# Attention with head mixing and two gated layers on one core: attention's result kept in SBUF as operands, and another order of scores and loads

## The chip, the cores and the metric

One core of one Trainium2 chip. The time is device microseconds (us) of one execution, from the median of the runs; less is better. All arithmetic is fp32; the second stage splits each fp32 operand into a high and a low fp32r part and multiplies three times.

## The reference, cut to what matters

```
scores = q @ k.T / 8                       # 4 batches, 12 heads, 448 rows, head size 64
scores = einsum('bhij,hg->bgij', scores, w_pre)
attn = exp(scores - max); attn /= sum(attn) + 1e-9
attn = einsum('bhij,hg->bgij', attn, w_post)
x = (attn @ v) as [1792 tokens, 768]
x = (sigmoid(x @ w_gate) * (x @ w_val)) @ w_out      # d_ff 1536
out = relu(x @ w_in2) ** 2 @ w_out2                  # d_ff 2048
```

## The kernel before

**Attention** (`attention`, L64) goes through 17 row tiles, of 60 rows (the first), 100 or 120 rows, four to a batch (five in the first). A tile has a step for each 20 rows: 3, 5 or 6 steps, 92 in all. The *scores* of a tile are computed per head pair (six pairs p): TensorE writes `turn`, ScalarE copies it to `e` (L211), and two DMAs (L215) spread `e` into the tile `g`, in which rows and heads lie as the head mixing wants them. All twelve DMAs into `g` must land before the next tile's first *premix* (L226, TensorE, `g` to `ps_m`). A step is: premix, maximum (L242, VectorE), exponent (L250, ScalarE, one step later), normal (L258), postmix (L277, TensorE, three steps later, copied into `ap` by VectorE, L295). The *values* of a tile (L312, two halves of three head pairs) come in the fourth and fifth step of the next tile. The scores of tile n+1 are placed among the steps of tile n by the numbers `spread`. There are two PSUM tiles `turn`, used in turn by scores, postmix and values.

`valued` (L321) copies the values' result to `xo` (L326) and stores it in the DRAM tensor `xs` (L328). Loads are on SP's queue as well: `q_load` (L182), `k_load` (L178, one tile a head pair) and `v_load` (L190, half of a batch's heads in one DMA). SP issues its DMAs in order.

**The second stage** (`mlp`, L671) multiplies 2x2 block matrices with 7 products instead of 8. Its weights come as raw 64-bit words, are turned into the block combinations (`convert`: loads L761, ScalarE L765 and L768, VectorE L771, GpSimd L777, combinations L799, stores L806 to DRAM, here `gv`, `wo`, `wi`) in 34 *groups*, and are loaded again as units of six blocks (L856) which ScalarE and VectorE split (L872, L875) for TensorE (`job`, L901: 1430 jobs of three matmuls). The first 12 groups, `gv`, are those of w_gate and w_val; the first 252 jobs use one for each 21 jobs. Operand parts of x are made by L885 and L888; x itself is read from `xs` by `stored` (L976).

**What sets the order.** `Feed` is a planner that runs when the program is built: every task has a due job number, costs per engine and buffers from `Stock`s, and tasks are written into the engines' queues between the steps of attention (`feed.step`) and, after it, until all are out (`feed.finish`). A group may begin once `hold` jobs are out:

```
hold = max(0, min((count[0] - BEFORE) * PACE, need))
```

`cells` are buffers of 128x448; `widen` gives more of them as attention's pools close (`after_scores`, `after_mixes`, `after_all`).

Of the kernel before, what the change touches and what calls it, by code (L numbers as in the profile page):

```python
# [25 lines left out]
LAG = 3  # L26
NA = 4
EB = 4
KB = 10
UT = 6  # L30


# [28 lines left out]
    return rows  # L61


def attention(tc, feed, q, k, v, w_pre, w_post, xs, B, H, S, D):  # L64

# [30 lines left out]
    def last_of(n):  # L98
        return n + 1 == NT or tiles[n + 1][0] != tiles[n][0]

    with ExitStack() as ctx, ExitStack() as mix, ExitStack() as low, ExitStack() as left:
        kw = dict(side="right")
        one = ctx.enter_context(tc.tile_pool(name="a_one", bufs=1, **kw))
        pv = ctx.enter_context(tc.tile_pool(name="a_v", bufs=4, **kw))
        po = ctx.enter_context(tc.tile_pool(name="a_o", bufs=2, **kw))
        pa = ctx.enter_context(tc.tile_pool(name="a_a", bufs=NA, **kw))
        pg = low.enter_context(tc.tile_pool(name="a_g", bufs=1, **kw))
        ps_t = ctx.enter_context(tc.tile_pool(name="ps_t", bufs=1, space=PSUM, **kw))
# [69 lines left out]
        def k_load(b, p):  # L178
            k_t[b, p] = pk.tile([P, S], F32, tag="k", name="k")
            nc.sync.dma_start(out=k_t[b, p], in_=k[b, p])  # L180

        def q_load(n, p0=0, p1=NP):  # L182
            if p0 == 0:
                q_t[n] = p2.tile([P, NP, IM], F32, tag="q", name="q")
            n0, isz = sum(sizes[:n]) * H * D, sizes[n]
            n1 = n0 + isz * H * D
            x = q[n0:n1].rearrange("(d p i) -> d p i", d=P, p=NP)
            nc.sync.dma_start(out=q_t[n][:, p0:p1, :isz], in_=x[:, p0:p1])

        def v_load(b, i):  # L190
            v_t[b, i] = pv.tile([P, 2 * VP, JT, D], F32, tag="v", name="v")
            nc.sync.dma_start(out=v_t[b, i], in_=v[b, i])

        def scores(n, p, ps, early=False):
# [107 lines left out]
        def values(n, i):  # L302

            b, i0, i1, length, lead = tiles[n]
            c = length * GI
            ps = next_turn()
            x = mixed_of(n).rearrange("p (j y g) c -> p j y g c", y=2, g=H)
            vt = v_t[b, i]
            for m in range(VP):
                for j in range(JT):  # L310
                    for o in range(2):
                        nc.tensor.matmul(  # L312
                            ps[o * D : (o + 1) * D, 0, m * 2 * c : (m + 1) * 2 * c],
                            lhsT=vt[:, 2 * m + o, j],
                            rhs=x[:, j, :, (i * VP + m) * 2 + o],
                            start=j == 0,
                            stop=j == JT - 1,
                        )
            return lambda: valued(n, i, ps)

        def valued(n, i, ps):  # L321
            b, i0, i1, length, lead = tiles[n]
            w = i1 - i0
            xo = po.tile([P, VP, IM], F32, tag="xo", name="xo")
            x = ps[:, 0, : VP * length * STEP].rearrange("p (m w) -> p m w", m=VP)[:, :, lead : lead + w]
            nc.scalar.copy(xo[:, :, :w], x)  # L326
            to = xs[b][i * VP * P : (i + 1) * VP * P, i0:i1].rearrange("(m p) n -> p m n", p=P)
            nc.sync.dma_start(out=to, in_=xo[:, :, :w])  # L328
            if last_of(n) and (i + 1) * VP == NP:
                feed.fire(("x", b))  # L330


        plan = {s: [] for s in range(NS + 12)}
        for n in range(1, NT):
            s0, s1 = starts[n - 1], starts[n]
            spread = {3: (1, 1, 0), 5: (2, 2, 1, 1, 0), 6: (2, 2, 1, 1, 0, 0)}[s1 - s0]
            p = NP - sum(spread)
            for m, x in enumerate(spread):
                for _ in range(x):
                    plan[s0 + m].append(("scores", n, p))  # L340
                    p += 1
# [18 lines left out]
            scores(1, p, next_turn())  # L360
        q_load(2)

        k_next = {}
        for n in range(NT):
            if not last_of(n) or n + 1 == NT:
                continue
            b = tiles[n][0] + 1
            first_free = KB - NP
            for p in range(NP):
                at = starts[n - 1] + 1 + p // 2 if p < first_free else starts[n - 1] + 2 + p // 2  # L370
                k_next.setdefault(at, []).append((b, p))
        v_next = {2: [(0, 0)], 3: [(0, 1)]}
        for n in range(NT):
            if last_of(n) and n + 1 < NT:
                v_next[starts[n] + 2] = [(tiles[n + 1][0], 0)]
                v_next[starts[n] + 3] = [(tiles[n + 1][0], 1)]

        closed = False
        for s in range(NS + 12):
            if s < NS:  # L380
                premix(s)
            if 2 <= s < NS + 2:
                normal(s - 2)
            if s < NS:
                maximum(s)
            if 1 <= s <= NS:
                exponent(s - 1)
                if s == NS:
                    mix.close()
                    low.close()  # L390
                    feed.widen(1)
                    feed.free["PE"] = feed.now
            after = []
            if LAG <= s < NS + LAG:
                after.append(postmix(s - LAG))
            for x in k_next.get(s, ()):
                k_load(*x)
            for x in v_next.get(s, ()):
                v_load(*x)
            units = plan[s]  # L400
            for f, *x in units:
                if f == "values":
                    after.append(values(*x))
                    while len(after) > 1:
                        after.pop(0)()
            for f, *x in units:
                if f == "scores":
                    if after:
                        after.pop(0)()
                    n, p = x  # L410
                    scores(n, p, next_turn())
                    if p == NP - 1 and n + 2 < NT:
                        q_load(n + 2)
                    if n == NT - 1 and p == NP - 1:
                        left.close()
                        closed = True
                        feed.widen(0)
            for f in after:
                f()
            if 3 <= s < NS:  # L420
                feed.step(3.8)
            elif s >= NS:
                feed.step(1.5)
# [3 lines left out]
LAT = 0.15  # L427
FAR = 2.0
SLOW = 8.0
BEFORE = 12  # L430
PACE = 34
MARGIN = 1.5
PRODUCTS = ("a1", "d5", "b6", "a2", "b7", "d3", "b4")
OUTER = ("y2", "x1", "x6", "x7", "x4", "z5", "z3")
# [49 lines left out]
class Feed:  # L484
# [53 lines left out]
    def gate(self, key):  # L538
        t = Task(None, (), 0, 0)
        self.writer[key] = self.gates[key] = t  # L540

    def fire(self, key):
        t = self.gates.pop(key)
# [124 lines left out]
SP = ("SP", 0.36, False)  # L668


def mlp(ctx, tc, xs, wg, wv, wo, wi2, wo2, out):  # L671

# [1 line left out]


    feed = Feed(tc)
    NX, N = len(xs), xs[0].shape[1]
    DM = out.shape[0]  # L680
    KD = DM // P
    tiles = {"wg": wg, "wv": wv, "wo": wo, "wi2": wi2, "wo2": wo2}
# [6 lines left out]
    def pool(name, bufs, **kw):  # L689
        return ctx.enter_context(tc.tile_pool(name=name, bufs=bufs, reuse_waits="tile", **kw))  # L690
# [5 lines left out]
        for _ in range(n):  # L696
            feed.stock(cells, pool(f"m_c{feed.count}", 1, side="left"), 1)

    feed.stock(raws, pool("m_r", 2, side="left"), 2)
    feed.stock(ys, pool("m_y", 2, side="left"), 2)  # L700
    widen(10)
    dram = pool("m_dram", 1, space=DRAM)

    def after_scores():
        widen(12)
        feed.stock(w32s, pool("m_w30", 2, side="left"), 2)
        feed.stock(ws, pool("m_w0", 1, side="left"), 1)

    def after_mixes():
        feed.stock(w32s, pool("m_w31", 1, side="left"), 1)  # L710
        feed.stock(ws, pool("m_w1", 1, side="left"), 1)
        widen(20)
        for n in range(4):
            feed.stock(seeded if n < 2 else banks, pool(f"m_ps{n}", 1, space=PSUM, side="left"), 1)

    def after_all():
        feed.stock(ws, pool("m_w2", 1, side="left"), 1)
        widen(49)
        for n in range(4, 8):
            feed.stock(banks, pool(f"m_ps{n}", 1, space=PSUM, side="left"), 1)  # L720

    feed.wide = [after_scores, after_mixes, after_all]
    KG = max(K1, K2)
    spill = [dram.tile([KG * P, 2 * N], F32, name=f"spill{i}") for i in range(2)]

    def cell(dtype=F32):
        return Buf(cells, [P, N], dtype, "c")

    for b in range(NX):
        feed.gate(("x", b))  # L730


    count = [0]
# [429 lines left out]
    def middle(m, c, o):  # L1163
        x2[m, c] = o

    layer(lambda m, c, need: stored(xs[c], ("x", c), m, 0, need), gated, gv, so, K1, spill[0], 16, middle, True)
    layer(
        lambda m, c, need: x2[m, c],
        squared,
# [11 lines left out]
@with_exitstack  # L1181
def whole(ctx, tc, q, k, v, w_pre, w_post, wg, wv, wo, wi2, wo2, out):
    B, H, S, D = k.shape[0], 2 * k.shape[1], k.shape[3], k.shape[2] // 2
    DM = out.shape[0]
    dram = ctx.enter_context(tc.tile_pool(name="dram", bufs=1, space=DRAM))
    xs = [dram.tile([DM, S], F32, name=f"xs{b}") for b in range(B)]
    with tc.manual_schedule():
        feed = mlp(ctx, tc, xs, wg, wv, wo, wi2, wo2, out)
        attention(tc, feed, q, k, v, w_pre, w_post, xs, B, H, S, D)
        feed.finish()  # L1190


# [50 lines left out]
```

## Time and profile before

| | us |
|---|---|
| median of 3 runs | 1404.83 (1395.96 to 1408.46) |
| the profiled execution | 1398.87 |
| its span, first to last instruction | 1397.1 |

The page gives busy time by engine, the span in 40 slices, waits and the chain that ended last. TensorE has work in 89% of the span, but the first third is attention with many short matmuls and waits, and the rest is one long stream of 4290 matmuls of the second stage. A difference of about 1% (14 us) is what a measurement of this kernel can tell from no change.

### The profile page before, as it was taken

The numbers are of one execution on the slowest core, as the hardware profiler recorded it, in microseconds if no ns is written. First come the engines' busy times: TensorE is split into PE (matmuls) and PEld (weight loads), VectorE is DVE, ScalarE is ACT, GpSimd is POOL, SyncE is SP. The second block draws the span as 40 slices with busy tenths as digits, with TensorE's granted clock in tenths as the row PEclk, the third lists the DMA queues.
The fourth block names the chain that finished last, engine by engine and source line by source line (L and its number), as shares of the span: only waits on it lengthen the run. The fifth ranks groups of instructions, "written<-read, shape, count | busy, mean of one in ns | idle before, by whom it ended". The sixth has DMA issues, their size and how long they took to land.

```text
span 1397.1 us, 31155 instructions
## 1 busy us (share of the span) xinstructions
PE 1249.2 (89%) x12474; PEld 1043.0 (75%) x12474; DVE 879.2 (63%) x1399; ACT 736.6 (53%) x1351; POOL 288.9 (21%) x380
## 2 busy tenths in 40 slices
PE   4786787778688799999999999999999999999998
PEld 1454455545356678798899889999888999999998
DVE  2464465556366665568756599957688556898612
ACT  3564465455466454566555664764556435436620
POOL 3132222233233222321323300123313000000000
PEclk8898898999899999999999999999999999999999
DMA  5667657776676558788678861266775534352222
GB/s 152 192 220 215 193 190 233 227 208 211 187 234 217 170 194 289 243 272 273 224 268 271 281 195 57 64 219 194 266 270 175 156 110 144 99 161 57 57 85 79
DMA packets 138540, 263.93 MB, mean 189 GB/s; under 512 B 31964, under 2 KB 87836, under 8 KB 138396
## 3 DMA queue, kind: packets, MB, share of 16 engines
q1 hardware_dynamic: 137786, 261.39, 58.8%
q8 instruction: 98, 1.61, 0.5%
q10 hardware_dynamic: 610, 0.55, 0.1%
q14 instruction: 46, 0.38, 0.1%
HBM read 157.64 MB, written 64.68 MB: 159 GB/s over the span
## 4 chain that ended last, share of the span: by engine, by line
PE 58%; DVE 3%; ACT 1%; issue 1%; DMA 1%; DVEq 0%; SPq 0%; ACTq 0%
PE ps L901 58%; DVE w L875 2%; DVE c L917 1%; ACT w L872 1%; DVE c L888 0%; DMA wo<-y 0%; DMA w<-wi 0%; ACT raw L765 0%; DMA spill<-c 0%; ACT c L885 0%; DVE c L1052 0%; ACT c L925 0%; ACT ps L925 0%; ACT c L927 0%; DVE y L771 0%
## 5 line engine op out<-in xcount | busy, mean ns | idle before, releaser
L901 PE MATMUL ps<-c,w 128*128 128x448 f32 x4290 | 890.9, 369 | 24.4 <-DVE w L875 11.2
L901 PEld LDWEIGHTS ps<-c,w 128*128 128x128 f32 x4290 | 808.9, 189 | 105.4 <-DVE w L875 19.5
L875 DVE TENSOR_TENSOR w<-w,w 128x768 fp32r<-128x768 f32 x189 | 193.4, 1027 | 173.3 <-ACT w L872 169.7
L777 POOL TENSOR_TENSOR y<-y,raw 128x384 int32<-128x384 int32 x136 | 153.4, 1149 | 430.6 <-DVE y L771 156.5
L872 ACT CAST w<-w 128x768 fp32r<-128x768 f32 x189 | 156.8, 833 | 135.6 <-PE ps L901 118.6
L242 DVE TENSOR_REDUCE nm<-ps_m 128x2 f32<-128x896 f32 (+1 forms) x92 | 98.4, 1070 | 173.8 <-PE ps_m L226 173.4
L888 DVE TENSOR_TENSOR c<-c 128x448 fp32r<-128x448 f32 x280 | 166.1, 637 | 26.1 <-ACT c L885 23.0
L885 ACT CAST c<-c 128x448 fp32r<-128x448 f32 x280 | 144.0, 566 | 58.9 <-DVE c L917 52.4
L226 PE MATMUL ps_m<-g,wp 64*64 64x448 f32 (+1 forms) x720 | 96.7, 594 | 84.8 <-DMA gv<-y 26.2
L917 DVE TENSOR_TENSOR c<-ps,c 128x448 f32<-128x448 f32 x172 | 106.4, 622 | 88.5 <-PE ps L901 65.6
L211 ACT COPY e<-turn 120x896 f32<-120x896 f32 (+1 forms) x96 | 86.8, 908 | 136.6 <-issue 63.5
L277 PEld LDWEIGHTS turn<-wn,a 64*64 64x64 f32 x5040 | 113.7, 145 | 53.8 <-issue 49.7
L262 POOL TENSOR_SCALAR wn<-wq,sm 128x60 f32<-128x60 f32 x180 | 75.2, 432 | 334.7 <-DVE sm L259 232.9
L203 PE MATMUL turn<-k,q 64*64 64x448 f32 (+3 forms) x776 | 106.1, 603 | 18.0 <-DVE ap L295 12.2
L277 PE MATMUL turn<-wn,a 64*64 64x60 f32 x5040 | 113.5, 233 | 7.5 <-issue 7.5
L226 PEld LDWEIGHTS ps_m<-g,wp 64*64 64x64 f32 (+1 forms) x720 | 25.3, 141 | 123.4 <-issue 85.4
L250 ACT ACTIVATE a<-ps_m,nm 128x448 f32<-128x448 f32 x180 | 113.0, 640 | 6.9 <-DVE nm L242 6.1
L917 DVE TENSOR_TENSOR c<-c 128x448 f32<-128x448 f32 x184 | 112.8, 646 | 2.2 <-PE ps L901 0.6
L295 DVE COPY ap<-turn 128x960 f32<-128x960 f32 x88 | 101.4, 1152 | 19.7 <-PE turn L277 19.2
L925 ACT COPY c<-ps 128x448 f32<-128x448 f32 x128 | 67.6, 533 | 72.9 <-PE ps L901 70.1
L312 PE MATMUL turn<-ap,v 128*64 128x120 f32 (+2 forms) x1632 | 84.6, 261 | 1.3 <-DVE ap L295 1.3
L312 PEld LDWEIGHTS turn<-ap,v 128*64 128x64 f32 x1632 | 77.4, 139 | 4.0 <-DVE ap L295 1.4
(40 smaller groups left out, 491.8 us busy)
## 6 DMA issues: line engine op xcount, KB each, us to landing
w<-gv SPq DMA_DIRECT2D x84, 384.0 KB
g<-e SPq DMA_DIRECT2D x108, 210.0 KB
raw<-in_wo SPq DMA_DIRECT2D x56, 384.0 KB
w<-wi SPq DMA_DIRECT2D x56, 384.0 KB
w<-wo SPq DMA_DIRECT2D x49, 384.0 KB
wo<-y SPq DMA_DIRECT2D x42, 384.0 KB
g<-e SPq DMA_DIRECT2D x84, 175.0 KB
gv<-y SPq DMA_DIRECT2D x36, 384.0 KB
```

The lines of the kernel that those rows point to most:

```text
L203: nc.tensor.matmul(ps[c:c1, o, :S], lhsT=q_t[n][r, p, c:c1], rhs=kt[r], start=True, stop=True)
L226: nc.tensor.matmul(ps[u * HP : (u + 1) * HP, y, :S], lhsT=wp[r], rhs=g_of[n % 2][r, 2 * t + u], start=True, stop=True,)
L250: nc.scalar.activation(a[:, y], ps[:, y, :S], AF.Exp, bias=nm[:, y : y + 1], accum_out=sm[:, y : y + 1])
L277: nc.tensor.matmul(out[c : c + HP, u, j // 2, y], lhsT=a[r, y, j * HP : (j + 1) * HP], rhs=wn[r, y].rearrange("p g i -> p (g i)"), start=True,
L312: nc.tensor.matmul(ps[o * D : (o + 1) * D, 0, m * 2 * c : (m + 1) * 2 * c], lhsT=vt[:, 2 * m + o, j], rhs=x[:, j, :, (i * VP + m) * 2 + o] ...
L777: e.tensor_tensor(out=y3, in0=y3, in1=of(raw.tile.bitcast(I32)[:, :, 0])[:, i], op=ALU.add)
L872: e.copy(dst.tile[:, 0], flat())
L875: e.tensor_tensor(out=dst.tile[:, 1], in0=flat(), in1=dst.tile[:, 0].bitcast(F32), op=ALU.subtract)
L885: e.copy(hi.tile, src.tile)
L888: e.tensor_tensor(out=lo.tile, in0=src.tile, in1=hi.tile.bitcast(F32), op=ALU.subtract)
L901: e.matmul(bank.tile, lhsT=a[k], rhs=x[l], start=start and n == 0, stop=stop and n == 2, skip_group_check=more,)
L917: e.tensor_tensor(out=out.tile, in0=a.tile, in1=b.tile, op=op)
```

## The change

Attention's result no longer goes through DRAM. Each head pair of each batch has a `cells` buffer of its own (24 of them) from the first tile of its batch (`Feed.take`); `valued` writes into it by three ScalarE copies for each half where one went to `xo`, and the second stage's operand tasks read these buffers as their source. `xs`, its 34 stores and the 24 loads of x are gone.

The scores of the next tile stand two a step in each tile's first three steps. Loads of k and v are issued in the fourth step and later, after the step's scores; v comes in six DMAs a batch of 256 KB instead of two of 768 KB. A tile of q lies in one piece per partition (100-row tiles had six pieces of 400 B). The k pool has 9 buffers instead of 10, the v pool 8 smaller ones.

Of the planner's numbers, `BEFORE` goes from 12 to 8, `PACE` from 34 to 30, the first planned step from 3 to 9. At the start there is one buffer for raw weights and one for their combinations (two before), the second of each comes at `after_scores`; the cells at the start are 27 (10), then 4 (12), 18 (20) and 42 (49) more: 91 as before, of which x holds up to 24.

```diff
-KB = 10
+KB = 9
+VB = 8
...
+                x = p2.tile([P, NP * IM], F32, tag="q", name="q")
+                q_t[n] = x[:, : NP * sizes[n]].rearrange("p (h i) -> p h i", h=NP)
...
         def v_load(b, i):
-            v_t[b, i] = pv.tile([P, 2 * VP, JT, D], F32, tag="v", name="v")
+            v_t[b, i] = pv.tile([P, 2, JT, D], F32, tag="v", name="v")
...
-            nc.scalar.copy(xo[:, :, :w], x)
-            to = xs[b][i * VP * P : (i + 1) * VP * P, i0:i1].rearrange("(m p) n -> p m n", p=P)
-            nc.sync.dma_start(out=to, in_=xo[:, :, :w])
+            for m in range(VP):
+                to = feed.x[b][i * VP + m]
+                if i0 == 0:
+                    feed.take(to)
+                nc.scalar.copy(to.tile[:, i0:i1], x[:, m])
+                if last_of(n):
+                    feed.fire(to)
...
-            spread = {3: (1, 1, 0), 5: (2, 2, 1, 1, 0), 6: (2, 2, 1, 1, 0, 0)}[s1 - s0]
+            spread = (2, 2, 2) if n > 1 else (2,)
...
             for p in range(NP):
+                loads[starts[n - 3 + p // 3] + 3 + min(p % 3, starts[n - 2 + p // 3] - starts[n - 3 + p // 3] - 4)].append((k_load, b, p))
+            for i in range(NP):
+                loads[starts[n] + 3 + i // 2].append((v_load, b, i))
...
-            if 3 <= s < NS:
+            for f, *x in loads[s]:
+                f(*x)
+            if 9 <= s < NS:
                 feed.step(3.8)
...
-BEFORE = 12
-PACE = 34
+BEFORE = 8
+PACE = 30
...
+    def take(self, b):
+        del b.stock.line[bisect_left(b.stock.line, b.serial)]
+        _, _, b.pool = heapq.heappop(b.stock.free)
+        shape, dtype, name = b.make
+        b.tile = b.pool.tile(shape, dtype, tag="x", name=name)
...
+    feed.x = [[Buf(cells, [P, N], F32, "x") for _ in range(KD)] for _ in range(NX)]
...
-    layer(lambda m, c, need: stored(xs[c], ("x", c), m, 0, need), gated, gv, so, K1, spill[0], 16, middle, True)
+    layer(lambda m, c, need: feed.x[c][m], gated, gv, so, K1, spill[0], 16, middle, True)
```

TensorE's queue from the third step to the fifth of the second tile of the second batch (six steps; L226 of before is L227 of after). Before:

```order
L226 MATMUL ps_m<-g_160,wp 64x448 x4
L277 MATMUL turn_163<-wn,a 64x60 x28
L203 MATMUL turn_162<-k,q 64x448 x2
L203 MATMUL turn_162<-k,q 56x448 x2
L226 MATMUL ps_m<-g_160,wp 64x448 x4
L277 MATMUL turn_163<-wn,a 64x60 x28
L312 MATMUL turn_162<-ap_156,v 64x120 x24
L203 MATMUL turn_163<-k,q 64x448 x2
L203 MATMUL turn_163<-k,q 56x448 x2
L226 MATMUL ps_m<-g_160,wp 64x448 x4
L277 MATMUL turn_162<-wn,a 64x60 x28
L312 MATMUL turn_162<-ap_156,v 64x120 x24
```

After:

```order
L227 MATMUL ps_m<-g_202,wp 64x448 x4
L278 MATMUL turn_205<-wn,a 64x60 x28
L204 MATMUL turn_204<-k,q 64x448 x2
L204 MATMUL turn_204<-k,q 56x448 x2
L204 MATMUL turn_205<-k,q 64x448 x2
L204 MATMUL turn_205<-k,q 56x448 x2
L227 MATMUL ps_m<-g_202,wp 64x448 x4
L278 MATMUL turn_204<-wn,a 64x60 x28
L312 MATMUL turn_205<-ap_198,v 64x120 x24
L227 MATMUL ps_m<-g_202,wp 64x448 x4
L278 MATMUL turn_204<-wn,a 64x60 x28
L312 MATMUL turn_205<-ap_198,v 64x120 x24
```

The sixth pair of scores (L203, now L204) has moved from behind the values of the fourth step to the third step.

SP's queue around the fifth tile of the first batch (the `10x12x448` DMAs are those into the g of the tile behind it). Before:

```order
L215 DMA g_161<-e 10x12x448 x8
L761 DMA raw<-in_wg 128x768 x2
L192 DMA v<-in_v 128x1536
L215 DMA g_161<-e 10x12x448 x2
L806 DMA gv_103<-y 128x384
L761 DMA raw<-in_wg 128x768 x2
L192 DMA v<-in_v 128x1536
L328 DMA xs_57<-xo 128x3x100
L215 DMA g_161<-e 10x12x448 x2
L188 DMA q<-in_q 128x720
```

After:

```order
L189 DMA q<-in_q 128x720
L180 DMA k<-in_k 128x448 x3
L765 DMA raw<-in_wg 128x768 x2
L216 DMA g_203<-e 10x12x448 x12
L189 DMA q<-in_q 128x720
L216 DMA g_202<-e 10x12x448 x12
L189 DMA q<-in_q 128x600
L810 DMA gv_148<-y 128x384
L765 DMA raw<-in_wv 128x768 x2
L193 DMA v<-in_v 128x512 x4
```

The twelve DMAs into g now stand together, with the loads behind them.

SP's queue early in the second stage, at a place where weight groups are stored (L806, L810) and units of them loaded (L856, L860); `gv_103` to `gv_108` and `gv_148` to `gv_153` hold two groups each, in the order of use. Before:

```order
L856 DMA w_7042<-gv_104 128x768
L761 DMA raw<-in_wo 128x768 x2
L856 DMA w_7081<-gv_104 128x768
L806 DMA gv_108<-y 128x384
L761 DMA raw<-in_wo 128x768 x2
L806 DMA gv_108<-y 128x768 x2
L856 DMA w_7139<-gv_105 128x768
L806 DMA gv_108<-y 128x768
L856 DMA w_7159<-gv_105 128x768
```

After:

```order
L860 DMA w_7420<-gv_151 128x768
L765 DMA raw<-in_wg 128x768 x2
L810 DMA gv_152<-y 128x384
L860 DMA w_7449<-gv_151 128x768
L810 DMA gv_152<-y 128x768 x3
L860 DMA w_7498<-gv_151 128x768
L860 DMA w_7504<-gv_152 128x768
L765 DMA raw<-in_wv 128x768 x2
L860 DMA w_7552<-gv_152 128x768
```

Before, the last groups of `gv` are stored while units three tensors earlier are loaded; after, `gv_152` is read two rows behind its last store. In all, 40 raw loads (10 groups) stand ahead of the last DMA into g before, and 18 (four and a half groups) after.

## Rows read from the trace of the kernel before

**Rows 1.** The page: busy time of each engine.

```profile
PE 1249.2 (89%) x12474; PEld 1043.0 (75%) x12474; DVE 879.2 (63%) x1399; ACT 736.6 (53%) x1351; POOL 288.9 (21%) x380
```

**Rows 2.** Stretches: attention, then two of the second stage.

```profile
core 0: us, PE busy (x) PEld busy (x) DVE busy (x) ACT busy (x) POOL busy (x), PEclk, DMA share, GB/s
0.00:465.00 465.00, 346.37 (x7812) 223.37 (x7816) 247.41 (x429) 247.85 (x532) 134.26 (x244) 0.89 0.67 206
...
510.00:630.00 120.00, 113.42 (x531) 101.10 (x530) 72.93 (x105) 66.68 (x103) 35.31 (x31) 0.97 0.83 277
640.00:797.00 157.00, 154.76 (x750) 139.69 (x748) 102.86 (x147) 94.67 (x147) 47.65 (x41) 1.00 0.78 259
```

**Rows 3.** Line L226 (premix) until 470 us: TensorE waited for (us, times).

```profile
  DMA gv<-y: 26.2, 4
  DMA q<-in_q: 15.8, 3
...
  DMA k<-in_k: 11.0, 2
  DMA g<-e: 10.8, 1
  DMA c<-xs: 3.3, 2
  DMA raw<-in_wg: 2.8, 1
```

**Rows 4.** TensorE in order of time (start, us, instructions, idle time before).

```profile
90.83 0.93 PE L226 MATMUL ps_m<-g,wp 64*64 64x448 f32 x8
...
94.84 0.93 PE L226 MATMUL ps_m<-g,wp 64*64 64x448 f32 x8
...
97.30 0.98 PE L226 MATMUL ps_m<-g,wp 64*64 64x448 f32 x8
...
101.44 0.97 PE L203 MATMUL turn<-k,q 64*64 64x448 f32 x8
102.23 0.93 PE L226 MATMUL ps_m<-g,wp 64*64 64x448 f32 x8
...
112.81 1.01 PE L226 MATMUL ps_m<-g,wp 60*64 60x448 f32 x2 [6.23 <-DMA k<-in_k]
...
118.29 0.93 PE L226 MATMUL ps_m<-g,wp 64*64 64x448 f32 x8
```

**Rows 5.** Stretches of the tile after that, columns as in rows 2.

```profile
120.00:126.00 6.00, 5.40 (x127) 2.47 (x122) 4.27 (x9) 4.13 (x10) 1.20 (x3) 1.00 0.58 185
...
134.00:138.00 4.00, 0.00 (x0) 0.00 (x0) 0.00 (x0) 0.98 (x4) 0.15 (x1) 0.88 1.04 267
138.00:142.00 4.00, 0.00 (x0) 0.00 (x0) 0.00 (x0) 0.00 (x0) 0.00 (x0) 0.50 1.03 354
```

**Rows 6.** SP's queue in the same stretch: start, time of the issues, DMAs.

```profile
118.26 7.34 SPq L215 DMA_DIRECT2D g<-e  x8
...
127.28 1.05 SPq L192 DMA_DIRECT2D v<-in_v  x1
...
135.48 2.14 SPq L215 DMA_DIRECT2D g<-e  x2
```

**Rows 7.** ScalarE's copies of the values' result, by form (count, busy, mean ns, idle before).

```profile
L326 ACT COPY xo<-turn 128x360 f32<-128x360 f32 x18 | 8.2, 458 | 34.9 <-PE turn L312 34.9
...
L326 ACT COPY xo<-turn 128x180 f32<-128x180 f32 x2 | 0.6, 308 | 6.4 <-PE turn L312 6.4
```

**Rows 8.** Line L771 alone (two for each weight group): us, DVE busy, clock, DMA share, GB/s.

```profile
0.00:450.00 450.00, 11.16 (x20) 0.89 0.67 205
...
640.00:797.00 157.00, 8.86 (x16) 1.00 0.78 259
```

**Rows 9.** The page: a DMA issue, its count and size.

```profile
w<-gv SPq DMA_DIRECT2D x84, 384.0 KB
```

More of the change, by code (lines that the diff above doesn't have):

```diff
@@ L61, in row_order, with attention @@
     return rows
-def attention(tc, feed, q, k, v, w_pre, w_post, xs, B, H, S, D):
+def attention(tc, feed, q, k, v, w_pre, w_post, B, H, S, D):
     nc = tc.nc
@@ L103, in attention @@
         one = ctx.enter_context(tc.tile_pool(name="a_one", bufs=1, **kw))
-        pv = ctx.enter_context(tc.tile_pool(name="a_v", bufs=4, **kw))
-        po = ctx.enter_context(tc.tile_pool(name="a_o", bufs=2, **kw))
+        pv = ctx.enter_context(tc.tile_pool(name="a_v", bufs=VB, **kw))
         pa = ctx.enter_context(tc.tile_pool(name="a_a", bufs=NA, **kw))
@@ L183, in q_load @@
             if p0 == 0:
-                q_t[n] = p2.tile([P, NP, IM], F32, tag="q", name="q")
+                x = p2.tile([P, NP * IM], F32, tag="q", name="q")
+                q_t[n] = x[:, : NP * sizes[n]].rearrange("p (h i) -> p h i", h=NP)
             n0, isz = sum(sizes[:n]) * H * D, sizes[n]
@@ L187, in q_load @@
             x = q[n0:n1].rearrange("(d p i) -> d p i", d=P, p=NP)
-            nc.sync.dma_start(out=q_t[n][:, p0:p1, :isz], in_=x[:, p0:p1])
+            nc.sync.dma_start(out=q_t[n][:, p0:p1], in_=x[:, p0:p1])
         def v_load(b, i):
-            v_t[b, i] = pv.tile([P, 2 * VP, JT, D], F32, tag="v", name="v")
+            v_t[b, i] = pv.tile([P, 2, JT, D], F32, tag="v", name="v")
             nc.sync.dma_start(out=v_t[b, i], in_=v[b, i])
@@ L307, in values @@
             x = mixed_of(n).rearrange("p (j y g) c -> p j y g c", y=2, g=H)
-            vt = v_t[b, i]
             for m in range(VP):
@@ L313, in values @@
                             ps[o * D : (o + 1) * D, 0, m * 2 * c : (m + 1) * 2 * c],
-                            lhsT=vt[:, 2 * m + o, j],
+                            lhsT=v_t[b, i * VP + m][:, o, j],
                             rhs=x[:, j, :, (i * VP + m) * 2 + o],
@@ L323, in valued @@
             w = i1 - i0
-            xo = po.tile([P, VP, IM], F32, tag="xo", name="xo")
             x = ps[:, 0, : VP * length * STEP].rearrange("p (m w) -> p m w", m=VP)[:, :, lead : lead + w]
-            nc.scalar.copy(xo[:, :, :w], x)
-            to = xs[b][i * VP * P : (i + 1) * VP * P, i0:i1].rearrange("(m p) n -> p m n", p=P)
-            nc.sync.dma_start(out=to, in_=xo[:, :, :w])
-            if last_of(n) and (i + 1) * VP == NP:
-                feed.fire(("x", b))
+            for m in range(VP):
[5 more added lines that the diff above has]
+                    feed.fire(to)
         plan = {s: [] for s in range(NS + 12)}
@@ L361, in attention @@
         q_load(2)
[L363 to L368, printed above, removed]
-            for p in range(NP):
[L370 to L376, printed above, removed]
+        loads = {s: [] for s in range(NS + 12)}
+        for i in range(NP):
+            loads[1 + i // 3].append((v_load, 0, i))
+        firsts = [n for n in range(1, NT) if tiles[n][0] != tiles[n - 1][0]]
+        for n in firsts:
+            b = tiles[n][0]
+            for p in range(NP):
+                loads[starts[n - 3 + p // 3] + 3 + min(p % 3, starts[n - 2 + p // 3] - starts[n - 3 + p // 3] - 4)].append((k_load, b, p))
+            for i in range(NP):
+                loads[starts[n] + 3 + i // 2].append((v_load, b, i))
         closed = False
@@ L395, in attention @@
                 after.append(postmix(s - LAG))
[L396 to L399, printed above, removed]
             units = plan[s]
@@ L668, with mlp @@
 SP = ("SP", 0.36, False)
-def mlp(ctx, tc, xs, wg, wv, wo, wi2, wo2, out):
+def mlp(ctx, tc, NX, N, wg, wv, wo, wi2, wo2, out):
     feed = Feed(tc)
-    NX, N = len(xs), xs[0].shape[1]
     DM = out.shape[0]
@@ L697, in widen @@
             feed.stock(cells, pool(f"m_c{feed.count}", 1, side="left"), 1)
-    feed.stock(raws, pool("m_r", 2, side="left"), 2)
-    feed.stock(ys, pool("m_y", 2, side="left"), 2)
-    widen(10)
+    feed.stock(raws, pool("m_r0", 1, side="left"), 1)
+    feed.stock(ys, pool("m_y0", 1, side="left"), 1)
+    widen(27)
     dram = pool("m_dram", 1, space=DRAM)
     def after_scores():
-        widen(12)
+        feed.stock(raws, pool("m_r1", 1, side="left"), 1)
+        feed.stock(ys, pool("m_y1", 1, side="left"), 1)
+        widen(4)
         feed.stock(w32s, pool("m_w30", 2, side="left"), 2)
@@ L711, in after_mixes @@
         feed.stock(ws, pool("m_w1", 1, side="left"), 1)
-        widen(20)
+        widen(18)
         for n in range(4):
@@ L717, in after_all @@
         feed.stock(ws, pool("m_w2", 1, side="left"), 1)
-        widen(49)
+        widen(42)
         for n in range(4, 8):
@@ L723, in mlp @@
     KG = max(K1, K2)
+    feed.x = [[Buf(cells, [P, N], F32, "x") for _ in range(KD)] for _ in range(NX)]
+    for x in feed.x:
+        for b in x:
+            feed.gate(b)
     spill = [dram.tile([KG * P, 2 * N], F32, name=f"spill{i}") for i in range(2)]
@@ L727, in cell @@
         return Buf(cells, [P, N], dtype, "c")
-    for b in range(NX):
-        feed.gate(("x", b))
     count = [0]
@@ L1183, in whole @@
     B, H, S, D = k.shape[0], 2 * k.shape[1], k.shape[3], k.shape[2] // 2
-    DM = out.shape[0]
-    dram = ctx.enter_context(tc.tile_pool(name="dram", bufs=1, space=DRAM))
-    xs = [dram.tile([DM, S], F32, name=f"xs{b}") for b in range(B)]
     with tc.manual_schedule():
-        feed = mlp(ctx, tc, xs, wg, wv, wo, wi2, wo2, out)
-        attention(tc, feed, q, k, v, w_pre, w_post, xs, B, H, S, D)
+        feed = mlp(ctx, tc, B, S, wg, wv, wo, wi2, wo2, out)
+        attention(tc, feed, q, k, v, w_pre, w_post, B, H, S, D)
         feed.finish()
@@ L1214 @@
     vt = np.concatenate([v, np.zeros((B, H, JT * P - S, D), v.dtype)], axis=2)
-    vt = vt.reshape(B, 2, H // 2, JT, P, D).transpose(0, 1, 4, 2, 3, 5)
+    vt = vt.reshape(B, H // 2, 2, JT, P, D).transpose(0, 1, 4, 2, 3, 5)
     laid = {
```

## The prediction

> **What bounds the kernel now.** I read the page first [rows 1]: TensorE is busy for 1249.2 of 1397.1 us, so about 148 us of idle time are all that a new order alone can win, and a little more where TensorE ran at its slower clock. The stretches say where they lie [rows 2]: in attention TensorE is busy for 346 of 465 us at a mean granted clock of 0.89; later it is busy for 154.76 of 157 us at 1.00. So the second stage is bound by TensorE's own matmuls, and attention by something else.
>
> The waits name it [rows 3]. The first premix of a tile waits 69.9 us in all for DMAs, in 13 waits (26.2 + 15.8 + 11.0 + 10.8 + 3.3 + 2.8). The names are those of whatever landed last beside it: what the premix needs is g. The order of time shows one such end of a tile [rows 4]. The last scores of the tile behind it start at 101.44 and take 0.97, the fifth step starts at 102.23, and the next tile's premix at 112.81, after 6.23 of idleness. From the end of those scores to that premix it is 10.4 us (copy by ScalarE, SP's issue, landing), and TensorE has work for little more than four of them (until 112.81 - 6.23 = 106.58). At the end of the tile after it, from 134 to 142 us, the DMAs are saturated, 1.04 and 1.03 of 16 engines busy, while the compute engines stand nearly still [rows 5], and SP's queue shows why [rows 6]: eight DMAs into g, then loads of raw weights and of v (two of 768 KB), and the last g DMAs only at 135.48, behind them.
>
> **The change part by part.** All terms are set against the profiled execution, 1398.9 us (a span of 1397.1 and 1.8 around it); the median of the runs shown is 6 us (0.4%) above it.
>
> *Waits for g.* The last scores move from the fourth step to the third, and loads of k and v are issued behind all twelve DMAs into g. Steps of one tile [rows 4]: 94.84 to 97.30 (third) and 97.30 to 102.23 (fourth, 4.93). The last scores now end about where the fourth step begins, and the fourth step and the fifth, with values in both, lie between them and the next tile: 4.93 less one score, 0.79 (101.44 to 102.23), is 4.1 for the fourth, and as much for the fifth, 8 to 9 us; six-step tiles have their sixth besides. Against a chain of 10.4 us, which was measured with loads ahead of it, a short wait is left in five-step tiles and none in six-step ones. I take 1 us for each of the 13 waits, and 4 more as an allowance for the first tile, which the start's loads still press on: 69.9 becomes 17, a gain of 53. Its bounds are 70 (nothing left) and, if the DMAs are as crowded as before, about half, 35.
>
> [...]
>
> *The steps themselves.* The third step has two scores instead of one: 4.01 instead of 2.46, +1.55. The fourth loses one: -0.79. Fifteen tiles pay 0.76: +11 us. Second scores wait a little for VectorE's copy of the same PSUM tile, which the 4.01 holds already.
>
> *Three copies where one was.* By the two forms shown [rows 7] a copy costs (458 - 308) / 180 = 0.83 ns a column, so 120 columns cost 258 ns and three of them 774, 316 ns more than now; 34 halves make 11 us of ScalarE. They are queued in the fourth and fifth steps, where ScalarE sat idle for 34.9 us ahead of the 18 large copies alone, waiting for the values' matmuls. I cost them at nothing; if exponents stood waiting behind them, at 11 us at most.
>
> *No xs.* 34 stores and 24 loads leave SP's queue and the DMAs; they paid no wait of their own except 3.3 us (in the first term). In the second stage x was loaded ahead of its use.
>
> *Fewer groups beside attention.* This is the part that can cost. By the order, 18 raw loads (four and a half groups) stand ahead of the last DMA into g, where it was 40 (ten). So seven and a half gv groups must be made while TensorE goes through the first 252 jobs. It uses a group in 63 matmuls: at 157 / 750 = 0.209 us each [rows 2] that is 13.2 us, and a unit of weights (18 matmuls) is 3.8 us. In the queue shown for after, the last raw loads of gv stand about four units apart, so the order wants a group in 15 us. The trace made 16 / 2 = 8 groups in 157 us, 19.6 us each [rows 8], while TensorE did not wait. If that is the pace, five such intervals fall 23 us behind; three buffers of loaded units are about 11 us ahead, and 12 us remain. Bounds: below, nothing, since the pace of before was the planner's own (34 jobs of three matmuls are 21.3 us) and not shown to be the chip's; above, the 23 and as much again for SP, whose queue holds loads of units behind stores that wait. I take 12, the row's own pace.
>
> Sum: 1398.9 - 53 - 16 + 11 + 12 = 1353 us.
>
> [...] Between 120 and 126 us almost nothing but DMAs into g was in flight [rows 5, 6]: 185 GB/s, with 0.58 of the engines busy. Twelve DMAs of 10 x 12 x 448 x 4 bytes are 2.58 MB, at that rate 13.9 us, against 12.0 for three steps: they were spread over four steps, and now stand closer than they can move.
> [...]
>
> **The rivals.** *First: the waits vanish and the weights keep up.* For it: in six-step tiles there are 11 us behind the last scores, and the second stage moved 277 GB/s at a share of 0.83 [rows 2], so there is some room. Against: 13 waits with six different names are not likely to go to the last one. Time: 1398.9 - 70 - 16 + 11 = 1324.
>
> *Second: the DMAs into g are themselves the limit.* They need 13.9 us in a five-step tile of some 21, and what q, k, v and weights left over runs ahead of them. Half of the waits and half of the slow steps stay: 1398.9 - 35 - 8 + 11 + 12 = 1379. Against it: the saturated stretch was full of v, raw weights, stores and short q pieces, and xs and half of the weights leave attention.
>
> *Third, on the other side: TensorE starves for weights at the start of the second stage.* The place is the last store of a gv group, on which the load of its unit and every DMA behind it on SP wait. For it: units take 384 KB in 3.8 us [rows 9], 104 GB/s; the other 173 of the 277 GB/s were 20 us groups, and 15 us groups would want 231, in all 335, a share of 1.0. Beside attention a group took 450 / 10 = 45 us [rows 8]. Against it: 354 GB/s were moved for four microseconds [rows 5], and TensorE's stretch at 19.6 us a group had no wait. It decides from the point where a group takes so long that seven intervals cost more than the 58 us won: (c - 15) x 7 - 11 = 58 gives c = 25 us. At 30 us: 1398.9 - 58 + 94 = 1435.
>
> *That the change does not do what it says:* it does not in one point, eight groups beside attention, of which the order holds four and a half; that is in the sum.
>
> **How the numbers follow.** The forecast, 1353, with its own range of 1335 to 1370, 0.52. The first rival 0.22, the second 0.18, the third 0.08. 1% is about what a measurement of this kernel can tell from no change, 14 us of the median, so faster means below 1391. Forecast and first rival lie below, the second mostly (0.14 of 0.18, the rest the same), the third in part (0.01 faster, 0.02 the same, 0.05 slower): faster 0.89, same 0.06, slower 0.05. The range reaches from just below the first rival, 1318, to beyond the second, 1386, and leaves out the third and some at both ends.
>
> **What would show it right or wrong.** Right: the DMA-released waits of the premix fall from 69.9 to below 20 us, first steps of tiles take about 4.0 and not 5.5, third steps 4.0, attention's last premix comes 50 to 65 us earlier, and 252 jobs of the second stage show new waits for split weights (VectorE's w) of some 12 us. Wrong: waits of 3 us and more at tile ends with a DMA share near 1 (second rival); gaps in TensorE's stream at the sixth to twelfth gv group, with SP waiting on stores (third); third steps well above 4.0, or exponents late behind the three copies.

## The result, and the profile after

The kernel after takes 1350.89 us (median of 3 runs, 1349.84 to 1359.51), the kernel before 1404.83: a ratio of 0.965, 95% interval 0.955 to 0.974. Measured again on another chip beside 11 runs of before it was 0.970 (0.967 to 0.972). The forecast was 1353. The profiled execution took 1349.84 us, 49.0 less than that of before. Its page answers to [rows 1]:

```profile
PE 1242.8 (92%) x12474; PEld 1036.0 (77%) x12474; DVE 889.0 (66%) x1409; ACT 739.4 (55%) x1419; POOL 291.4 (22%) x370
```

TensorE does the same work and is idle for 105 us instead of 148. Where the idle time went is read from stretches, attention first (its last premix starts at 401.5 instead of 465.2), then two of the second stage [rows 2]:

```profile
core 0: us, PE busy (x) PEld busy (x) DVE busy (x) ACT busy (x) POOL busy (x), PEclk, DMA share, GB/s
0.00:400.00 400.00, 333.79 (x7790) 212.18 (x7792) 235.54 (x406) 235.44 (x570) 107.12 (x215) 0.95 0.59 184
...
460.00:580.00 120.00, 109.55 (x521) 97.87 (x520) 75.55 (x111) 65.02 (x102) 34.92 (x27) 0.99 0.76 257
580.00:740.00 160.00, 157.63 (x765) 142.88 (x764) 103.72 (x144) 94.69 (x147) 48.10 (x41) 1.00 0.76 248
```

In attention TensorE's busy share rose from 0.74 to 0.83 and its mean granted clock from 0.89 to 0.95, while the DMAs moved less in each microsecond (184 GB/s for 206). The premix's waits, line L227, which was L226 [rows 3]:

```profile
L227 PE MATMUL ps_m<-g,wp x720: 533/536/1006, 25.2 to 401.5; 64*64 64x448 f32 x176, 60*64 60x448 f32 x4
its engine sat idle before it (us, times) until:
  ACT a L251: 9.7, 6
  DMA v<-in_v: 7.8, 1
  DMA k<-in_k: 3.8, 1
  DMA q<-in_q: 1.0, 1
  ACT x L329: 0.6, 1
```

The waits that DMAs ended fell from 69.9 to 12.6 us, and 7.8 of these belong to the end of the first tile, where it was 7.8 before as well. What a good tile end looks like now is seen in order of time at the same place as [rows 4]; TensorE first, the idle time in brackets:

```profile
96.29 0.98 PE L227 MATMUL ps_m<-g,wp 64*64 64x448 f32 x8
...
99.64 0.97 PE L204 MATMUL turn<-k,q 64*64 64x448 f32 x8 [0.56 <-DVE ap L296]
100.43 0.93 PE L227 MATMUL ps_m<-g,wp 64*64 64x448 f32 x8
...
104.43 0.98 PE L227 MATMUL ps_m<-g,wp 64*64 64x448 f32 x8
...
108.47 0.59 PE L227 MATMUL ps_m<-g,wp 60*64 60x448 f32 x2
...
112.42 0.93 PE L227 MATMUL ps_m<-g,wp 64*64 64x448 f32 x8
```

The last scores end at 100.6; the fourth and the fifth step fill the eight microseconds until the next tile's premix at 108.47, which waits for nothing, and that tile's first step takes 3.95 us. SP's queue beneath it (start, time of the issues, DMAs) has the twelve DMAs into g in one piece and all loads behind them [rows 6]:

```profile
92.10 11.49 SPq L216 DMA_DIRECT2D g<-e  x12
103.69 0.44 SPq L189 DMA_DIRECT2D q<-in_q  x1
104.18 1.83 SPq L180 DMA_DIRECT2D k<-in_k  x3
106.11 0.84 SPq L765 DMA_DIRECT2D raw<-in_wg  x2
```

One tile end earlier it does not go so. Two loads of raw weights, the first of the kernel, stand between the eighth and the ninth DMA into g:

```profile
65.83 7.13 SPq L216 DMA_DIRECT2D g<-e  x8
73.01 0.96 SPq L765 DMA_DIRECT2D raw<-in_wg  x2
74.08 3.35 SPq L216 DMA_DIRECT2D g<-e  x4
```

and TensorE stands still for 3.80 us, comes back at a lower clock (granted clock 0.50 from 86 to 92 us, 1.00 from 78 to 82; eight premix matmuls take 1.77 us and not 0.93), and the tile's first step takes 6.07 us:

```profile
78.09 0.98 PE L227 MATMUL ps_m<-g,wp 64*64 64x448 f32 x8
...
86.09 1.77 PE L227 MATMUL ps_m<-g,wp 64*64 64x448 f32 x8 [3.80 <-DMA k<-in_k]
...
92.16 0.93 PE L227 MATMUL ps_m<-g,wp 64*64 64x448 f32 x8
```

The releaser is named k, which was issued behind all of g. Nor were the DMAs into g issued late: SP was through with them at 77.43, 4.9 us before TensorE was ready (86.09 - 3.80 = 82.29), and at the good tile end just as long before (103.59 and 108.47). What differs is the two loads ahead of the last four: 768 KB, an estimated 3.4 us at the 229 GB/s that were moved from 78 to 82 us. Two of the last experiments act on this place.

The second stage, from its first job matmul to its last, became longer: 936.2 us for 920.7. Its longest waits, from 407 us on (total, times, longest), are for split weights; before they were 11.2 and 4.7 us:

```profile
PE ps L905 <- DVE w L879: 18.3, 15, 4.1
PE ps L905 <- ACT w L876: 5.5, 2, 3.7
```

So the account of the two profiled executions is: first job matmul at 407.5 instead of 472.4, 64.9 us won; 15.5 us lost behind it; 49 in all.

### The profile page after: what moved, and what is told of

The parts are those of the page before. It is cut to its first block, busy times and chain, and to the rows that moved or that the text cites. A ratio compares the mean times of both kernels' runs of the same rounds, so it can differ in the third digit from the quotient of the medians.

```text
span 1348.0 us, 31150 instructions
## 1 busy us (share of the span) xinstructions
PE 1242.8 (92%) x12474; PEld 1036.0 (77%) x12474; DVE 889.0 (66%) x1409; ACT 739.4 (55%) x1419; POOL 291.4 (22%) x370
## 4 chain that ended last, share of the span: by engine, by line
PE 57%; DVE 4%; DMA 2%; ACT 1%; issue 1%; POOL 0%; SPq 0%; DVEq 0%; ACTq 0%
PE ps L905 57%; DVE w L879 2%; DMA w<-gv 1%; DVE c L921 1%; DMA gv<-y 1%; ACT w L876 1%; DVE c L892 1%; DVE y L803 1%; DMA raw<-in_wg 0%; POOL y L781 0%; ACT raw L769 0%; ACT raw L772 0%; ACT c L931 0%; DVE y L775 0%; DVE c L1056 0%
## 5 line engine op out<-in xcount | busy, mean ns | idle before, releaser
L879 DVE TENSOR_TENSOR w<-w,w 128x768 fp32r<-128x768 f32 x189 | 196.8, 1046 | 159.4 <-ACT w L876 157.8
L781 POOL TENSOR_TENSOR y<-y,raw 128x384 int32<-128x384 int32 x136 | 161.7, 1211 | 506.2 <-DVE y L775 180.9
L892 DVE TENSOR_TENSOR c<-c 128x448 fp32r<-128x448 f32 x250 | 151.4, 653 | 13.7 <-ACT c L889 11.9
L889 ACT CAST c<-c 128x448 fp32r<-128x448 f32 x250 | 128.5, 566 | 50.6 <-DVE c L921 46.2
L278 PEld LDWEIGHTS turn<-wn,a 64*64 64x64 f32 x5040 | 104.5, 137 | 47.7 <-issue 41.1
L204 PE MATMUL turn<-k,q 64*64 64x448 f32 (+3 forms) x776 | 104.2, 589 | 30.1 <-DVE ap L296 23.8
L227 PE MATMUL ps_m<-g,wp 64*64 64x448 f32 (+1 forms) x720 | 90.8, 565 | 23.5 <-ACT a L251 9.7
L278 PE MATMUL turn<-wn,a 64*64 64x60 f32 x5040 | 105.1, 223 | 4.8 <-issue 2.3
L921 DVE TENSOR_TENSOR c<-c 128x448 f32<-128x448 f32 x160 | 95.5, 631 | 2.4 <-PE ps L905 0.6
L204 PEld LDWEIGHTS turn<-k,q 64*64 64x64 f32 (+3 forms) x776 | 24.7, 133 | 74.4 <-DVE ap L296 56.6
```

What stands on the lines that cost most here:

```text
L204: nc.tensor.matmul(ps[c:c1, o, :S], lhsT=q_t[n][r, p, c:c1], rhs=kt[r], start=True, stop=True)
L278: nc.tensor.matmul(out[c : c + HP, u, j // 2, y], lhsT=a[r, y, j * HP : (j + 1) * HP], rhs=wn[r, y].rearrange("p g i -> p (g i)"), start=True,
L781: e.tensor_tensor(out=y3, in0=y3, in1=of(raw.tile.bitcast(I32)[:, :, 0])[:, i], op=ALU.add)
L879: e.tensor_tensor(out=dst.tile[:, 1], in0=flat(), in1=dst.tile[:, 0].bitcast(F32), op=ALU.subtract)
L889: e.copy(hi.tile, src.tile)
L892: e.tensor_tensor(out=lo.tile, in0=src.tile, in1=hi.tile.bitcast(F32), op=ALU.subtract)
```

## The experiments

In the table "stage" is the time from the first to the last job matmul, "waits" the premix's waits that DMAs ended, both from the profiled execution. The median and the ratio to the kernel before, measured on the same chip, are from all runs.

| kernel | last premix | waits | stage | median | ratio (95%) |
|---|---|---|---|---|---|
| before | 465.2 | 69.9 | 920.7 | 1404.8 | 1 |
| before, new scores | 437.0 | 39.2 | 920.6 | 1379.7 | 0.989 (0.981-0.997) |
| before, new loads | 454.7 | 43.3 | 919.7 | 1386.1 | 0.990 (0.986-0.994) |
| before, both | 426.4 | 21.2 | 923.0 | 1349.0 | 0.965 (0.960-0.971) |
| both, after's groups | 408.6 | 19.1 | 949.1 | 1366.9 | 0.978 (0.975-0.982) |
| after | 401.5 | 12.6 | 936.2 | 1350.9 | 0.965 (0.955-0.974) |
| after, again | 401.4 | 13.2 | 935.6 | 1356.0 | 0.970 (0.967-0.972) |
| after, old scores | 415.2 | 24.9 | 939.3 | 1367.4 | 0.976 (0.973-0.980) |
| after, hold 26 | 403.9 | 11.5 | 930.7 | 1351.6 | 0.967 (0.964-0.970) |
| after, old planner | 406.1 | 15.0 | 931.3 | 1349.7 | 0.967 (0.962-0.973) |
| after, no groups | 381.9 | 6.9 | 949.0 | 1369.3 | 0.981 (0.976-0.986) |
| after, late groups | 396.4 | 9.5 | 930.1 | 1340.5 | 0.960 (0.957-0.962) |
| late, hold 26 | 396.0 | 11.7 | 929.5 | 1338.0 | 0.958 (0.956-0.960) |

### One half of the change at a time

The kernel before with the new places of the scores alone:

```diff
-            spread = {3: (1, 1, 0), 5: (2, 2, 1, 1, 0), 6: (2, 2, 1, 1, 0, 0)}[s1 - s0]
+            spread = (2, 2, 2) if n > 1 else (2,)
```

> The kernel before with only the scores moved (two a step in the first three steps). Theory A (the waits come from where the last scores and the loads stand in the order): about half of the 69.9 us of DMA-released premix waits goes, the loads still stand among the DMAs into g; 11 us come on top for the steps: first matmul of the second stage at about 445 us (472 before), time about 1378 us. Theory B (the waits come from the bytes in flight: xs, short q pieces and ten weight groups): waits stay above 55 us, first matmul of the second stage at 470 us or later, time 1395 us or more.

Measured: 1379.7 us, a ratio of 0.989; last premix 28 us earlier, first job matmul at 443.4, and 39.2 us of DMA-ended waits left: theory A. Its four runs lie 25 us apart (1369.8 to 1394.8), and three of them are 1.1 to 2.2% below the 1400.5 of before on that chip.

The kernel before with the loads of k and v behind the scores' DMAs, in the fourth step and later:

```diff
-            for x in k_next.get(s, ()):
-                k_load(*x)
-            for x in v_next.get(s, ()):
-                v_load(*x)
...
+            for f, *x in loads[s]:
+                f(*x)
```

> The kernel before with only the k and v loads moved behind the scores of the fourth and later steps. Theory A: the last scores stay late, so five-step tiles still wait; waits fall to about 40 us, first matmul of the second stage at about 440 us, time about 1370 us. Theory B: waits stay above 55 us, time 1390 us or more.

Measured: 1386.1 us, 0.990, between the two expectations; 43.3 us of waits left, and 11.1 more in three waits that the profile can put down to nothing.

Both edits together:

> The kernel before with both moves, and still xs in DRAM and ten weight groups beside attention. Theory A: nearly all of the gain in attention is here, waits 15 to 25 us, first matmul of the second stage at about 415 us, and the second stage is as before: time about 1345 us. Theory B: waits 45 us or more, time 1380 us or more.

Measured: 1349.0 us, 0.965 (the profiled execution took 1361.4, the three others 1347.5 to 1349.7, so its row of the table is some 12 us above its median). The waits, 21.2 us, are as theory A has them, but the first job matmul came at 432.7 and not at about 415. By the ratios one half wins 1.1%, the other 1.0%, both 3.5%, more than their sum. The profiled executions do not bear this out: there the last premix comes 28.2, 10.5 and 38.8 us earlier, which simply adds up. So that the halves need each other is not shown; that either alone leaves some 40 us of waits is. By the order, earlier scores alone still find loads ahead of g in the queue, and later loads alone leave the last scores near to the end of the tile. With x still in DRAM and ten groups beside attention this kernel is as fast as the kernel after, so the two moves are the gain, and the rest of the change nets about nothing.

The kernel after with the old places of the scores:

```diff
-            spread = (2, 2, 2) if n > 1 else (2,)
+            spread = {3: (1, 1, 0), 5: (2, 2, 1, 1, 0), 6: (2, 2, 1, 1, 0, 0)}[s1 - s0]
```

> The changed kernel with the scores back in their old places (two, two, one, one). Theory A: waits come back in five-step tiles, 25 to 35 us instead of 12.6, against 11 us won in the steps: first matmul of the second stage at 410 to 420 us (407.5 in the changed kernel), time 1352 to 1365 us. Theory B: with the bytes gone the old places do as well, waits stay at 13 to 18 us, the steps win 11 us: time about 1342 us.

Measured: 0.976, against 0.965 and 0.970 of the kernel after; the waits double to 24.9 us, and 10.5 more stand in three waits that the profile can put down to nothing. The first job matmul (421.1) and the time (1367.4) are just above theory A's ranges.

### x in SBUF, and the groups it leaves room for

The kernel with both moves, x through DRAM, and weight groups as in the kernel after:

```diff
-            if 3 <= s < NS:
+            if 9 <= s < NS:
...
-BEFORE = 12
-PACE = 34
+BEFORE = 8
+PACE = 30
...
-    feed.stock(raws, pool("m_r", 2, side="left"), 2)
-    feed.stock(ys, pool("m_y", 2, side="left"), 2)
+    feed.stock(raws, pool("m_r0", 1, side="left"), 1)
+    feed.stock(ys, pool("m_y0", 1, side="left"), 1)
...
     def after_scores():
+        feed.stock(raws, pool("m_r1", 1, side="left"), 1)
+        feed.stock(ys, pool("m_y1", 1, side="left"), 1)
```

> The kernel before with both moves (scores and loads) and with the weight groups as in the kernel after: one buffer each of raw weights and products until the scores are done, groups from the tenth step on, holds as in the kernel after. x still goes through DRAM. It differs from the kernel after in x alone. Theory A (the groups make the difference between the two moves alone and the kernel after, both in attention and in the second stage; x through DRAM costs little): attention's last premix at 400 to 405, second stage 933 to 940, 1349 to 1356. Theory B (x kept in SBUF shortens attention): last premix 410 to 416, 1360 to 1368. Theory C (x kept in SBUF takes SBUF and so delays weights): second stage 920 to 926, 1336 to 1342.

Measured: 1366.9 us, 0.978. The time lies in theory B's range, but the way to it is none of the three: attention is 7 us longer than in the kernel after (last premix 408.6, short of B's 410), the stage 13. The expectation is wrong in one point: this kernel differs from the kernel after in more than x. It still has q in six pieces for 100-row tiles, v in two DMAs a batch, ten k buffers and ten cells at the start. What follows for x in SBUF holds for x together with these; no run separates them. From here two steps of about the same size lead to the same time: ten groups for five and a half (0.978 to 0.965, 18 us), or x in SBUF (0.978 to 0.965 or 0.970, 12 to 19 us). In the profiles the ten groups make attention 17.8 us longer (426.4 for 408.6) and the stage 26.1 shorter (923.0 for 949.1); x in SBUF makes attention 7.1 and the stage 12.9 shorter. That explains the nothing: what x in SBUF wins is about what the second buffers for weights would have won, and the kernel after has these later and 17 more cells from the start. Whether both could be had was not tried. In the first 252 jobs TensorE sat idle for 22.1 us here and for 16.3 in the kernel after; loads of x and of units share SP's queue there, which is the likely reason and was not tried by itself.

### Is the second stage late because of the planner's hold?

The kernel after with a shorter hold, then with the planner's three numbers of before:

```diff
-PACE = 30
+PACE = 26
```

> The kernel after, with the planner's hold on weight groups loosened from 30 jobs a group to 26. Theory A (debt): the kernel after enters the second stage with five and a half groups where the kernel before had ten, and makes them there at 18 to 21 us each because that is what the chip and the order of the other work allow; the hold does not bind, so the second stage stays at 930 to 940 us from first to last job matmul and the time at 1345 to 1355. Theory B (hold): the groups after the twelfth are late because the hold keeps them back; the stage goes to 925 us or below and the time to 1335 to 1342.

```diff
-            if 9 <= s < NS:
+            if 3 <= s < NS:
...
-BEFORE = 8
-PACE = 30
+BEFORE = 12
+PACE = 34
```

> The kernel after with the planner's three numbers of before: groups beside attention from the fourth step on instead of the tenth, holds from the twelfth group in 34 jobs a group. By the order about three quarters of a group more is loaded before the last DMA into g. Theory A (debt, about 3 us of second stage for each missing group): second stage 930 to 936, attention as in the kernel after, 1345 to 1352. Theory B (the hold is what matters): holds end earlier up to group 38, so the waits at jobs 420 to 500 shrink and the stage goes below 928, 1338 to 1344.

Measured: 1351.6 and 1349.7 us, both 0.967. In the profiles both second stages are 5 us shorter, but the times are the same as after's. The hold is not what costs. With the planner's numbers of before, 20 raw loads stand ahead of the last DMA into g, for 18 in the kernel after and 40 before: these numbers are not what holds the groups back, and the single buffers for weights are the likely reason.

### What the groups cost attention

The kernel after without a group beside attention, then with the first begun at step 23 (the sixth tile) instead of step 9:

```diff
-            if 9 <= s < NS:
-                feed.step(3.8)
+            if s < NS:
+                pass
```

> The kernel after without any weight group beside attention; everything else alike. Theory A (the groups load attention, and a missing group is paid later): attention's last premix comes 5 to 15 us earlier than 401.5 because DMA queue, ScalarE and VectorE are free; the second stage cannot start until the first group is made, 25 to 35 us, and five and a half groups more are missing, 15 us: 1375 to 1395. Theory B (groups beside attention are free for attention): last premix at 400 to 402, and 1385 to 1405.

```diff
-            if 9 <= s < NS:
+            if 23 <= s < NS:
```

> The kernel after, with the first weight group begun at attention's step 23 (the start of the sixth tile) instead of step 9. Without any group the first five tiles ended 9.7 us earlier (120.6 against 130.3) and the last premix 19.6 us earlier; by that, groups cost attention time wherever they lie, and the first of them lies in five-step tiles that have no room. Theory A: the sixth tile starts at 119 to 123, the last premix comes at 391 to 396, about half a group is missing later (+1 to +2 us): 1340 to 1345, 6 to 10 below the kernel after on the same chip. Theory B: the cost only moves to the tiles behind, because the first group then crowds those: last premix 399 to 403, 1348 to 1353.

Without groups the last premix comes 19.6 us earlier, 381.9, more than I had expected, and 6.9 us of waits are left; but 42 us pass until the first job, and the time is 1369.3, below both ranges. With late groups attention is 5 us shorter and the stage 6, and the time is 1340.5, 15 us below the kernel after on the same chip (1356.0, the next run but one; 10 us between the profiled executions). SP's row at 73 us above says why the place matters: the loads that stand among g's DMAs there are not issued in the first five tiles any more (the first raw load goes out at 130.1 us, the sixth tile starts at 123.1). The premix's waits of that kernel:

```profile
  ACT a L251: 10.3, 6
  DMA v<-in_v: 6.1, 1
  DMA g<-e: 3.0, 2
  issue: 0.9, 1
  ACT x L329: 0.6, 1
  DMA k<-in_k: 0.4, 1
```

Of the waits that DMAs ended, only the first tile's (v, 6.1 us) is still a long one. That the stage is shorter too, with one group less begun by its first job (five for six), I had not expected. The gain lies in jobs 252 to 504, which take 156.4 us for 164.5, with 0.5 us of idle time for 5.9; I have no shown cause for it.

The same with the hold at 26:

> The same, with the planner's hold at 26 jobs a group instead of 30. The hold alone made no measurable difference (0.9671 against 0.9646 of the kernel before). If the hold does not bind (A), the time is that of the run with late groups alone within 3 us; if it binds once half a group more is missing (B), it is 4 to 8 us below that run.

Measured: 1338.0 us, 0.958 (0.956 to 0.960), within 3 us of the run before it. It is the fastest kernel of the study. Its attention runs at nearly the full clock (stretch, busy times, granted clock, DMA share, GB/s):

```profile
0.00:400.00 400.00, 335.61 (x7923) 214.49 (x7924) 235.91 (x408) 236.32 (x575) 104.74 (x215) 0.97 0.56 180
```

The kernel after on the same chip:

> The kernel after itself, unchanged, on the same chip as the two runs with late groups, so that a difference of 6 us can be told: 1346 to 1356, last premix at 400 to 406, second stage 930 to 938 us. Its spread shows how much of a difference in one profile is the run's own.

Measured: 1349.2 to 1358.6 in six runs, median 1356.0. Its profiled execution is the fastest of the six and shows 401.4 and 935.6 us, almost the numbers of the first profile.

## Why the prediction was right, point by point

**Waits for g: right.** 69.9 to 12.6 us was forecast as 17. The short waits in five-step tiles are fewer than one for each, and the first tile's is 7.8 us, where 4 were allowed. That the last scores must come earlier and the loads behind g is what the working said, and the runs with one of the two show it: 39.2 and 43.3 us remain. But the two moves alone do not give attention's whole gain. With them the last premix came at 426.4, 38.8 us earlier and not 63.7; fewer groups (408.6), then x in SBUF and what goes with it (401.5), brought the other 24.9, and the prediction had both at nothing for attention. The split is rough, since the profiled execution of the two moves is the slowest of its four.

**Slow steps behind a wait, 16 us of the sum: right in kind, too large.** I had counted eleven first steps at 1.5 us each, and no run shows these 16 us. What the runs show is 8.8: first steps, added up in order of time over 15 tiles (all but the first and the last), went from 77.5 to 68.7 us. Before, eleven of them, behind waits of 2.55 to 12.56 us, ran at a granted clock of 0.50 to 0.74 and took 5.56 us on average, and four, behind 2.13 us at most, ran at 1.00 and took 4.11; after, it is three (behind 7.83, 3.80 and 1.01 us) at 0.51 to 0.74 with 6.03, and twelve at 1.00 with 4.22. They take 4.6 us on average now, 5.2 before, so the sign "about 4.0 and not 5.5" is not met. Last steps lost what waits they held: 152.2 to 90.0 us from the fifth step to the end of the tile, 62 for a forecast of 53 from the waits alone.

**The steps' shape: right for the third, low for the fourth.** Third steps grew from 46.0 to 60.3 us (4.02 each, as forecast), and fourth steps shrank from 75.5 to 65.7, 0.65 each for 0.79. Net 4.5 us and not 11, because seven third steps of before were already above 3 us. Together attention was to be 58 us shorter, and its first job matmul came 64.9 us earlier.

**Three copies at nothing: right.** A copy of 120 columns takes 267 ns for the 258 worked out, and TensorE's waits for ScalarE's exponents fell (12.4 to 9.7 us) rather than rose:

```profile
L329 ACT COPY x<-turn 128x120 f32<-128x120 f32 x48 | 9.3, 267 | 34.9 <-PE turn L312 34.9
```

**No xs at nothing: wrong, and hidden by its counterpart.** At equal groups x in SBUF, with the other parts named above, is worth 12 to 19 us.

**Fewer groups, +12 us: near in size (15.5) by luck, wrong in place.** At x in DRAM the fewer groups cost the second stage 26.1 us, and x in SBUF with its parts gave 12.9 back; in time they cost 18 us and x won 12 to 19. The sum came out because one term was too small and the other, at nothing, left out a gain of the same size. The step of the working that failed is the five intervals that fall behind in the first 252 jobs. These took 189.2 us for 187.1, with 8.7 us of waits for split weights where before had 7.1. Groups were made there in 18.4 us (from the first raw load at 441.9 to that at 533.7, five groups on), not 19.6, and the loss is later: 4.5 us in jobs 252 to 504, and 9.0 in jobs 756 to 1092. The kernel after enters the stage four to five groups behind and stays behind (24 and a half groups through L775 when job 756 starts, 30 before): line L775, VectorE's part in a group, twice for each, alone in four stretches [rows 8]:

```profile
0.00:400.00 400.00, 5.51 (x10) 0.95 0.59 184
...
580.00:740.00 160.00, 8.91 (x15) 1.00 0.76 248
846.00:1127.00 281.00, 14.00 (x24) 0.98 0.72 232
```

Twelve groups are left for the stretch from 846 us on, where before made eight in the same microseconds, and there the two longest waits of the stage stand (3.69 us at 974, 4.07 at 1003.7). How far behind a kernel enters does not set this loss: the one without groups beside attention has 24 made when job 756 starts, and its jobs 756 to 1092 take 225.8 us, for 223.9 in the kernel after and 215.0 before. Idle time in the stage went from 22.4 to 33.7 us; the other 4 us are matmuls that run slower (370 ns on average for 369, at a granted clock of 0.98 in the stage for 0.99).

**The rivals.** The first (1324) needs both: waits all gone, and no loss in the second stage. Neither is the case, but the late groups move that way. The second (1379) fell: in the kernel without groups twelve DMAs into g went out in three steps, with a share of 0.60 between 105 and 117 us,

```profile
105.00:117.00 12.00, 10.80 (x286) 6.78 (x281) 7.02 (x14) 8.27 (x21) 2.11 (x5) 1.00 0.60 199
```

and the next tile (at 120.6) waited 0.8 us. So the DMAs move hardly faster than before (199 GB/s at a share of 0.60, for 185 at 0.58), but the eight microseconds behind the last scores are enough for them. The third (1435) fell by its own point: groups take 18.4 us there, not 25.

## What to carry to other kernels

A wait at the end of a stage that shows many different DMAs as releasers can come from one queue's order, as here: find the transfer that is needed, and move both its source earlier and what stands ahead of it later; either half alone left some 40 of 70 us of waits. Where a buffer is kept in SBUF, ask which work loses its room, and price both by an experiment that changes one of them. Background work is best begun where the foreground has slack: here one number, the step at which weight groups begin, was worth 15 us, about as much as x in SBUF with its parts.

## What I had not expected

Some five weight groups beside attention cost it 19.6 us, about 4 each, though no engine is full there (TensorE 0.83, VectorE 0.59, ScalarE 0.59 of the time); begun early, the first ones cost most: the first five tiles end at 130.3 us with them (127.1 in the kernel's second profile) and at 120.6 without.

The same kernel's runs can differ by 9 us on one chip (1349.2 to 1358.6 for the kernel after) where the kernel with late groups stays within 4 (1339.4 to 1342.9). Runs near such a difference are only told apart side by side.
